# Sketched attention with a phase-mixing MLP on one core: batch 3's queries turned by TensorE, the balance by sums on ScalarE, and a new order of work

## The chip, the core and the metric

The kernel runs on one core of one Trainium2 chip. The metric is the device time of one execution in microseconds (us). A core has five engines that each run their own instructions in order: TensorE (PE; its weight loads are listed apart as PEld), VectorE (DVE), ScalarE (ACT), GpSimd (POOL) and SyncE (SP, whose queue starts most of the transfers). An engine waits where an instruction needs something that another engine or a transfer has not finished; everything behind it on the same engine waits too.

## The reference

For each of 4 batches with 4 heads, 1088 tokens and 32 values per head:

```
phi(x)  = outer(S1 x, S2 x)              8 x 8 values per token
kv, z   = sum over tokens of phi(k) v^T, of phi(k)
x       = (phi(q) kv) / (phi(q) z + 1e-6)       heads side by side: 1088 x 128
theta   = x @ w_theta
y       = w_tok_r @ (x cos theta) + w_tok_i @ (x sin theta)    w_tok: 1088 x 1088
u       = x + y
out     = u + relu(u @ w_ch)
```

q, k, v are float32. The four w matrices come in float64, and the kernel reads their bits.

## The kernel before

**Stages.** k is rounded into two parts and summed into kv and z (batches 0, 1, then 2 and 3 together). q is loaded, scaled by a power of two, turned so that tokens lie along the free axis, rounded into f16 and a rest, and multiplied with the sketches (`levels`). VectorE builds denominators and outer products, TensorE makes the numerators, and ScalarE copies them from the accumulators into x, turned (`xT`). Then come theta, cosine and sine (ScalarE with its table), the products zr and zi (VectorE), the mixing with the 17 rows of w_tok (8 real, 8 imaginary, and a tail of both), and the last product with w_ch. Batches 0 and 1 are mixed row by row (`mix_row`, L1193); batches 2 and 3 go through seven products of half size (`winograd`, L1291) with sums and differences made by VectorE.

**Weights.** A row of w_tok is 1088 KB. It is loaded into a buffer of class "zs" (`weight`, L575). ScalarE makes two parts of it (L576 and L578), VectorE shifts one (L316) and adds them with a custom operation (L312). There are only 5 "zs" buffers, which the tiles of x also use.

**Queries.** `load` (L588 to L605) issues one transfer of 576 KB for batches 0 to 2. For batch 3, which stands in `QTURN`, it issues 16 transfers of 36 KB that put blocks of 32 tokens by 32 values in place, so that VectorE's transpose of 32x32 blocks (L944) turns the whole; ScalarE then scales it (L945). For the other batches `query_slices` turns three groups of three 128x128 blocks on TensorE (L951) and ScalarE scales each group out of the accumulator (L954).

**Turning x.** For batches 1 to 3, VectorE transposes xT in 32x32 blocks (L1097), one transfer writes it to memory (`far`, L1098) and four fetch it back (L1102).

**Balance.** Batches 2 and 3 are combined in one scheme, so batch 3 is scaled to batch 2's size by a power of two. `balance` (L1166) finds the largest magnitude in each of the two on VectorE (L1169), `ratio` makes the two powers from them with small VectorE operations, ScalarE scales batch 3 (L1092), and `add` (L1351) takes the scale back.

**Output.** `finish` (L1219) multiplies by w_ch, adds on VectorE, transposes there (L1240) and stores from several queues (L1236). The last part of batch 3's first half goes through `finish_turned` (L1266), which transposes on TensorE (L1274) and stores whole rows (L1286).

**The order.** No scheduler runs when the kernel is built. `ORDER` (L34) lists the numbers of all operations in the order in which they are issued, `GAPS` (L79) says ahead of which of them filler matmuls are put on TensorE (L361, results unused), and `SLOTS` (L80) gives each buffer its place in its class. Within an engine the instructions stand in this order; between engines only the operands decide. Helpers record nearly all matmuls at L332, VectorE's operations at L312, L316 and L319, so a line alone does not name an operation; the tiles do.

Of the kernel before, what the change touches and what calls it, by code (L numbers as in the profile page):

```python
# [18 lines left out]
ALU = mybir.AluOpType  # L19
# [12 lines left out]
RPS = 4  # L32
EARLY = (2, 60.0, 4.0)
ORDER = (  # L34
# [43 lines left out]
)  # L78
GAPS = {11: 3, 57: 3, 79: 3, 110: 1, 203: 8, 153: 1, 77: 5, 86: 2, 163: 1}  # L79
SLOTS = (  # L80
# [11 lines left out]
)  # L92
WARM = 0
LOAD_LEAD = 60.0
RAW_LEAD = 30.0
CHAINS = ((0,), (1,), (2, 3))
QPOOL = (False,) * 4
KEEP = (2, 3)
KEEP_CLS = "big"
PAIR = (2, 3)  # L100
QUADS = (2, 3)
QTURN = (3,)
XTURN = (1, 2, 3)
PARTS = ((0, 384), (384, 544))
APOOL = ()
# [140 lines left out]
def kernel(  # L246
# [81 lines left out]
    def vop(n, fn, w, r, due=None, two=False, lk=0):  # L328
        op("V", dve2(n) if two else dve(n), fn, w, r, due, lk=1 if two else lk)
# [836 lines left out]
    def balance():  # L1166
        at("even")
        for j, b in enumerate(PAIR):
            vop(NC * P, lambda j=j, b=b: V.tensor_reduce(out=even()[:, j:j + 1], in_=xT[b](), axis=AX.X, op=ALU.max,  # L1169
                                                         apply_absolute_value=True), [(even, j)], [xT[b]])  # L1170

        def ratio():
            e = even()
# [309 lines left out]
```

## Time and profile before

| what | value |
|---|---|
| median of 3 runs | 217.91 us (217.88 to 218.24) |
| the profiled execution | 217.77 us |
| its span in the profile | 216.0 us |
| mean granted clock of TensorE | 0.997 |
| read from memory, written | 29.84 MB, 4.00 MB |
| mean transfer rate over the span | 172 GB/s |

The profile shows one execution. Its span runs from the first to the last instruction that it records, and the execution's own time is 1.77 us longer. "Busy" counts the time in which at least one instruction of an engine runs, so overlapping matmuls count once: a group's busy time over its count is less than the mean duration of one. In rows of groups the columns are line, engine, operation, result and operands with their shapes, count, busy time, mean duration in ns, and the idle time just before with what ended it. In rows of the timeline they are start, length, engine, line, operation and count. A digit in the 40 slices is the busy share of a fortieth of the span in tenths.

### The profile page before, as it was taken

How to read it: one execution, taken by the hardware profiler on the slowest of the kernel's cores; microseconds unless marked ns; L12 is line 12 of the kernel's file. 1: busy time of each engine (PE TensorE's matmuls, PEld its weight loads, DVE VectorE, ACT ScalarE, POOL GpSimd, SP SyncE). 2: the span in 40 equal slices, each digit the busy share in tenths (PEclk: the TensorE clock that was granted, in tenths of full speed). 3: DMA queues.
4: the chain of work that ended last, by engine and by line, in shares of the span. 5: the costliest groups of instructions: out<-in, count | busy, mean ns of one | idle time of the engine just before them, and what ended most of it. 6: DMA issues, size and time to landing. Idle time of an engine off the chain costs nothing.

```text
span 216.0 us, 5299 instructions
## 1 busy us (share of the span) xinstructions
PE 207.4 (96%) x2140; PEld 150.2 (70%) x2140; DVE 180.7 (84%) x359; ACT 113.5 (53%) x240; POOL 38.5 (18%) x89
## 2 busy tenths in 40 slices
PE   7999999999999999999999999999999999999990
PEld 7777798968767666775656676576766776677660
DVE  1799999999999998998999999979497799955151
ACT  4899999999999896796711423159500000000000
POOL 1182640307300000930003010000220020020013
PEclk9999999999999999999999999999999999999998
DMA  6999999996996994192002244022660012110433
GB/s 226 395 417 418 380 362 420 429 324 143 347 244 230 421 429 177 56 323 49 0 0 36 40 141 113 0 39 108 137 109 0 0 39 50 17 36 4 76 62 67
DMA packets 28044, 37.06 MB, mean 172 GB/s; under 512 B 20564, under 2 KB 23044, under 8 KB 25844
## 3 DMA queue, kind: packets, MB, share of 16 engines
q1 hardware_dynamic: 22868, 31.86, 42.2%
q0 software_dynamic: 1552, 3.25, 7.1%
q10 hardware_dynamic: 3600, 1.62, 2.8%
q8 instruction: 17, 0.28, 0.5%
q14 instruction: 7, 0.06, 0.1%
HBM read 29.84 MB, written 4.00 MB: 157 GB/s over the span
## 4 chain that ended last, share of the span: by engine, by line
PE 58%; DMA 17%; DVE 10%; ACT 9%; issue 3%; SPq 1%; POOL 0%; POOLq 0%; DVEq 0%; ACTq 0%
PE ps L332 54%; DMA zs<-w_tok 11%; DMA zs<-far 2%; DMA st<-s 2%; DVE big L312 2%; ACT big L578 2%; PE ps L951 2%; ACT big L626 2%; DMA far<-zs 1%; DVE g L312 1%; PE ps L1053 1%; DVE big L316 1%; ACT g L726 1%; ACT big L576 1%; PE ps L361 1%
## 5 line engine op out<-in xcount | busy, mean ns | idle before, releaser
L332 PE MATMUL ps<-big,zs 128*128 128x384 f32 (+2 forms) x380 | 108.8, 435 | 0.0
L332 PEld LDWEIGHTS ps<-big,zs 128*128 128x128 f32 x380 | 67.1, 191 | 34.2 <-issue 0.9
L1281 ACT COPY g<-ps 80x256 f32<-80x256 f32 x1 | 0.4, 367 | 54.1 <-PE ps L1274 54.1
L332 PE MATMUL ps<-big,big 128*32 128x32 f32 (+2 forms) x352 | 21.8, 235 | 0.0
L312 DVE CUSTOM_DVE_ANT_0 big<-big,big 128x2176 uint16<-128x2176 uint16 x17 | 21.6, 1281 | 0.1
L578 ACT ACTIVATE big<-zs 128x1088 int32<-128x1088 uint32 (+1 forms) x18 | 21.3, 1190 | 0.7 <-DMA zs<-w_tok 0.7
L576 ACT ACTIVATE big<-zs 128x1088 f32<-128x1088 f32 x17 | 20.9, 1229 | 0.7 <-DMA zs<-w_tok 0.7
L332 PEld LDWEIGHTS ps<-big,big 128*32 128x32 f32 (+1 forms) x352 | 14.9, 125 | 5.6 <-issue 1.0
L312 DVE TENSOR_TENSOR big<-big,big 128x544 f32<-128x544 f32 x24 | 16.7, 713 | 0.1
L326 POOL DMA_DIRECT2D g<-big x6 | 5.3, 1070 | 56.0 <-ACT g L1213 56.0
L1236 POOL DMA_DIRECT2D out<-g x8 | 5.0, 631 | 50.3 <-DVE g L1240 36.0
L312 DVE TENSOR_TENSOR zs<-zs,g 128x384 f32<-128x384 f32 (+2 forms) x24 | 9.9, 449 | 4.0 <-DMA zs<-far 4.0
L316 DVE TENSOR_SCALAR big<-big 128x1088 int32<-128x1088 int32 x17 | 12.3, 721 | 0.0
L361 PE MATMUL ps<-idle 128*128 128x112 bf16 (+1 forms) x67 | 10.0, 312 | 1.3 <-POOL idle L363 1.3
L312 DVE TENSOR_TENSOR g<-lv 128x768 f32<-128x768 f32 x12 | 11.1, 950 | 0.1
L312 DVE TENSOR_TENSOR big<-big,hf 128x1152 f32<-128x1152 f32 x8 | 10.7, 1351 | 0.0
L332 PE MATMUL ps<-mf,big 128*128 128x96 f32 (+1 forms) x72 | 10.0, 278 | 0.4 <-DVE big L312 0.4
L332 PE MATMUL ps<-sbk,g 128*128 128x64 f32 x72 | 10.1, 276 | 0.3 <-ACT g L726 0.3
L332 PE MATMUL ps<-w,big 128*128 128x128 f32 (+1 forms) x76 | 10.2, 278 | 0.0
L332 PEld LDWEIGHTS ps<-w,big 128*128 128x128 f32 (+1 forms) x76 | 9.4, 190 | 0.5
L1139 ACT ACTIVATE g<-g 128x384 f32<-128x384 f32 x12 | 6.3, 532 | 6.7 <-DVE g L319 6.7
L332 PEld LDWEIGHTS ps<-sbk,g 128*128 128x128 f32 x72 | 9.0, 191 | 0.8 <-ACT g L726 0.6
(198 smaller groups left out, 353.0 us busy)
## 6 DMA issues: line engine op xcount, KB each, us to landing
zs<-w_tok SPq DMA_DIRECT2D x17, 1088.0 KB, 10.6
big<-k_l SPq DMA_DIRECT2D x5, 576.0 KB, 12.6
big<-v_l SPq DMA_DIRECT2D x4, 576.0 KB, 15.4
big<-q_l SPq DMA_DIRECT2D x3, 576.0 KB, 10.4
big<-hf POOLq DMA_DIRECT2D x3, 576.0 KB, 9.7
far<-zs SPq DMA_DIRECT2D x3, 576.0 KB, 3.8
zs<-far SPq DMA_DIRECT2D x12, 144.0 KB, 4.1
big<-k_l ACTq DMA_DIRECT2D x2, 576.0 KB, 4.2
```

Of the source, the lines that this page charges most:

```text
L312: eng.tensor_tensor(out=o, in0=a, in1=b, op=f)
L316: (eng or V).tensor_scalar(out=o, in0=a, scalar1=s1, scalar2=s2, op0=op0, **kw)
L326: op("G", 0.9, lambda: G.dma_start(dst(), src(), accum_op=ALU.add), w, r, fly=fly)
L332: T.matmul(o, lhs, rhs, start=start, stop=stop, skip_group_check=True)
L361: T.matmul(nowhere()[:, :n], idle()[:, 0:P], idle()[:, :n], start=True, stop=True, skip_group_check=True)
L576: op("A", 0.22 + n * 0.0009, lambda: A.activation(dfn(), words_of(raw(), n)[1].bitcast(F32), AF.Prelu, scale=2.0**-112, alpha=-(2.0**32)), ...
L578: op("A", 0.22 + n * 0.0009, lambda: A.activation(stp(), words_of(raw(), n)[0].bitcast(U32), AF.Copy, scale=2.0**-29), [stp], [raw])
L626: op("A", act(n) + 0.1, lambda: A.activation(flat(r()), kc(), AF.Square, accum_out=km()[:, 1:2]), [r, (km, 1)], [kx])
L726: op("A", act(GW), lambda kT=kT, tr=tr: A.copy(kT().rearrange("p c n -> p (c n)"), tr()), [kT], [tr])
L951: T.transpose(tr()[:, i * P:(i + 1) * P], x()[:, g * GC + i].rearrange("p h d -> p (h d)"), ident())
L1139: op("A", act(GW), lambda cs=cs: A.activation(cs()[:, 0], cs()[:, 1], AF.Abs), [(cs, 0)], [(cs, 1)])
L1236: E.dma_start(out[b, s0:s0 + n, f * SQ:(f + 1) * SQ].rearrange("(c j) i -> j c i", j=SQ), ot()[f * SQ:(f + 1) * SQ, :n].rearrange("j (c i) ...
```

## The change

Three things are changed, and one follows from them.

- `QTURN` is empty: batch 3's queries are loaded in one transfer of 576 KB and turned like those of the other batches, in three groups of three transposes on TensorE with a scaled copy by ScalarE behind each.
- `balance` takes the sum of magnitudes in place of the largest: ScalarE runs Abs over xT with an accumulator, and writes the magnitudes themselves, in bf16, into a buffer of class "hf" that nothing reads.
- `ORDER` and `SLOTS` are new. Operations are numbered anew, as batch 3's load is 1 operation in place of 4 and its turning 6 in place of 2. On every engine the instructions up to about 36 us of the trace stand as before. Behind that, all of the work of batches 0 and 1 up to theta is put ahead of the first mixing product (TensorE's 57.13 us in the trace of before), batch 1's turn of x comes earlier among VectorE's operations, and another part of the output comes last. `GAPS` names the same operations by their new numbers.

The lists cut to their first and last lines, and the rest whole:

```diff
 ORDER = (
-    0, 1, 29, 32, 4, 2, 5, 3, 34, 30, 356, 50, 33, 102, 44, 96, 6, 108, 103, 36, 7, 51, 366, 54, 144, 8, 97, 10, 9,
...
-    964, 988, 995, 921, 905, 996, 922, 997, 994, 1000, 916, 923, 998, 917, 924, 999, 918,
+    0, 1, 29, 32, 4, 2, 5, 3, 34, 30, 357, 47, 33, 99, 41, 93, 6, 105, 100, 36, 7, 48, 367, 51, 141, 8, 94, 10, 9, 11,
...
+    914, 965, 915, 916, 993, 996, 997, 994, 998, 1001, 920, 921, 922, 923, 999, 1000, 924, 925,
 )
-GAPS = {11: 3, 57: 3, 79: 3, 110: 1, 203: 8, 153: 1, 77: 5, 86: 2, 163: 1}
+GAPS = {11: 3, 54: 3, 76: 3, 107: 1, 200: 8, 150: 1, 74: 5, 83: 2, 160: 1}
...
-QTURN = (3,)
+QTURN = ()
...
     def balance():
         at("even")
         for j, b in enumerate(PAIR):
-            vop(NC * P, lambda j=j, b=b: V.tensor_reduce(out=even()[:, j:j + 1], in_=xT[b](), axis=AX.X, op=ALU.max,
-                                                         apply_absolute_value=True), [(even, j)], [xT[b]])
+            dump = buf("hf", (NC * P,), BF16, "dump")
+            op("A", act(NC * P) + 0.1, lambda j=j, b=b, dump=dump: A.activation(
+                dump(), xT[b](), AF.Abs, accum_out=even()[:, j:j + 1]), [dump, (even, j)], [xT[b]])
```

104 rows, old and new, of tables (ORDER, SLOTS) are left out of this document.

## The prediction

> **What bounds the kernel now.** I read the page first: its busy shares, its slices, and the engines of the chain that ended last.
>
> ```profile
> PE 207.4 (96%) x2140; PEld 150.2 (70%) x2140; DVE 180.7 (84%) x359; ACT 113.5 (53%) x240; POOL 38.5 (18%) x89
> PE   7999999999999999999999999999999999999990
> PEclk9999999999999999999999999999999999999998
> PE 58%; DMA 17%; DVE 10%; ACT 9%; issue 3%; SPq 1%; POOL 0%; POOLq 0%; DVEq 0%; ACTq 0%
> ```
>
> TensorE is busy for 207.4 of 216.0 us, in every slice but the first and the last, at the full clock throughout. So the bound is TensorE's own work, and time can be won in three places only: less of that work, the few waits inside it, and what lies behind its last matmul. The waits of TensorE from 18 us on, and then the chain in order of time, say how much there is of each.
>
> ```profile
> PE ps L332 <- DVE big L312: 0.4, 1, 0.4
> PE ps L332 <- ACT sm L783: 0.4, 1, 0.4
> PE ps L332 <- ACT g L726: 0.3, 1, 0.3
> ...
> 88.94 1.30 DVE zs L1097
> 90.25 3.05 DMA far<-zs
> ...
> 94.65 5.14 DMA zs<-far
> ...
> 117.78 90.94 PE ps L332 x515
> 208.94 0.72 PE ps L332 x6
> 210.44 0.52 DVE big L319
> 210.97 0.59 DVE g L1240
> 211.85 0.64 POOL out L1236
> 212.49 0.60 POOLq L1479
> ```
>
> Three idle spells of 0.3 to 0.4 us are all that the waits show, and from 117.78 us the chain is one piece of 515 matmuls. VectorE is nearly as full up to 120 us; the table by stage shows it, with ScalarE in the column behind.
>
> ```profile
> 36.00:57.00 21.00, 21.00 (x498) 17.32 (x488) 20.55 (x45) 20.18 (x49) 7.88 (x17) 1.00 0.92 321
> 57.00:70.00 13.00, 13.00 (x174) 8.58 (x163) 13.00 (x19) 12.34 (x21) 0.00 (x0) 1.00 0.86 247
> 100.00:120.00 20.00, 19.54 (x98) 12.72 (x97) 19.64 (x33) 7.96 (x12) 1.82 (x2) 1.00 0.12 20
> ```
>
> The columns are stretch and length, then PE, PEld, DVE, ACT and POOL busy. From 36 to 70 us VectorE is idle for 0.45 us and ScalarE for 1.5. TensorE is full, VectorE has no room, and whatever order is chosen has to keep both fed from each other.
>
> **The change, part by part.** The rows of the removed work and of its nearest relatives, grouped by form:
>
> ```profile
> L951 PE MATMUL ps<-ident,big 128*128 128x128 f32 x27 | 4.5, 283 | 0.0
> L954 ACT ACTIVATE big<-ps,qs 128x384 f32<-128x384 f32 x9 | 5.0, 602 | 0.0
> L944 DVE STREAM_TRANSPOSE big<-big 128x1152 f32<-128x1152 f32 x1 | 1.4, 1372 | 0.0
> L945 ACT ACTIVATE big<-big,qs 128x1152 f32<-128x1152 f32 x1 | 1.2, 1239 | 0.0
> L1169 DVE TENSOR_REDUCE even<-big 128x1 f32<-128x1152 f32 x2 | 2.7, 1330 | 0.8 <-ACT big L1081 0.8
> L924 ACT ACTIVATE big<-big 128x1152 f32<-128x1152 f32 x4 | 4.7, 1175 | 0.1
> L924 ACT ACTIVATION_READ_ACCUMULATOR big<-big 128x1 f32 x4 | 0.8, 201 | 0.0
> 20.64 0.48 PE ps L951 x3
> ```
>
> *Queries of batch 3 on TensorE.* VectorE loses one transpose, 1.37 us; ScalarE exchanges one copy of 1.24 us for three of 0.60, so +0.56. TensorE gains nine transposes. Their 27 relatives take 4.5 us of busy time, 167 ns each, so 1.5 us; three that stand alone on the chain take 0.48, so 1.44 for nine; between other matmuls the neighbours overlap them, and I know no bound below 1.0. TensorE is the bound and nothing hides them: I take **+1.3 us** (1.0 to 1.5). With no overlap at all it would be nine times the mean of 283 ns, 2.5 us; that stands as a rival below.
>
> [...]
>
> *The load.* Batch 3's queries came in 16 issues of 36 KB, and stand in SP's queue as follows.
>
> ```profile
> 36.75 14.23 SPq L596 DMA_DIRECT2D big<-q_l  x8
> 52.62 12.86 SPq L596 DMA_DIRECT2D big<-q_l  x8
> big<-q_l SPq DMA_DIRECT2D x3, 576.0 KB, 10.4
> big<-q_l SPq DMA_DIRECT2D x16, 36.0 KB, 10.6
> ```
>
> SP spends 27 us of its queue on them, with weight rows behind. One issue of 576 KB replaces them; its like land in 10.4 us. It now waits until TensorE has freed its buffer at about 37 us, and only two weight loads and later ones stand behind it; the data is used on TensorE from about 50 us, so I cost it at nothing. If it landed after 50 us, TensorE would wait from there.
>
> *Balance on ScalarE.* VectorE loses two reductions, 2.66 us; ScalarE gains two passes like L924's, 2 x (1.18 + 0.20) = 2.75 us. They stand behind the copies of the numerators of batches 2 and 3, where ScalarE has 12 us free in 20 (100 to 120 us). VectorE's total falls by 4.0 us and ScalarE's rises by 3.3. As VectorE is not the bound, this is worth what it removes of TensorE's waits, at most.
>
> *The order.* The instruction lists of the two programs agree up to TensorE's instructions at about 36 us, filler matmuls included. From there I added up each engine's list, each instruction at the spacing its form has in the trace of before, and compared when an operand is ready with when it is wanted. These are sums of rows followed by hand. One check is a row of before:
>
> ```profile
> 57.13 3.06 PE L332 MATMUL ps<-big,zs 128*128 128x384 f32 x9
> 78.70 0.25 PE L332 MATMUL ps<-sq,sm 32*32 32x16 f32 x8 [0.37 <-ACT sm L783]
> 117.78 1.33 PE L332 MATMUL ps<-mf,big 128*128 128x96 f32 x10 [0.42 <-DVE big L312]
> 209.49 0.86 PE L332 MATMUL ps<-big,w 128*128 128x384 f32 x2
> ```
>
> The sum puts before's first mixing product at 57.05 us, the row has 57.13. Over the whole list TensorE's sum ends at 207.2 us and the last row at 210.35: 3.2 us more, of which I put 1.4 to long matmuls that drift and 1.8 to waits, the two shown above (0.37, 0.42) and shorter ones whose idle time the profile fills with pipelined ends. Both parts of this split are estimates (waits 0.8 to 3.2).
>
> In the changed kernel all work of batches 0 and 1 up to the phase angles comes ahead of the first mixing product, which the sum puts at 68.7 us without waits, 70.5 with them. No mixing product fills gaps between 36 and 70 us, so TensorE waits where chains pass through VectorE or ScalarE: for the row scale behind the first denominators (wanted at 40.7, ready at 41.6), for the first outer products (0.2), and for batch 1's last numerators (0.2): **+1.35 us** of new waits (0.5 to 3). Behind that every operand is ready by the sums 1 to 2 us before it is wanted, the weight rows and batch 1's x too, so before's **1.8 us** of waits go. What is late next is VectorE, with those 1 to 2 us of slack.
>
> *The end.* Before, the last product is 384 wide, and a VectorE pass, a transpose and two stores issued by POOL one after the other follow it: from 210.35 to the span's end, 5.65 us. In the changed kernel a half of 160 columns comes last, finished by two short transposes, products of 80x256 and one VectorE pass of 0.42 us, with one store on each queue; by the landing of such a store I put this tail at 4.15 us, **-1.5 us** (-2.0 to 0).
>
> **The sum.** Profiled run 217.77 us (216.0 of span, 1.77 around it, which I leave as it is; 0.14 under the median of 217.91): +1.3 transposes +1.35 new waits -1.8 old waits -1.5 tail = -0.65, **217.1 us**. The likeliest case's own range, by the ends of the small terms, is 216.5 to 217.4. A measurement of this kernel can tell about 0.2%, 0.44 us, from no change.
>
> **The rivals.**
> - *The fill runs dry (slower).* Place: TensorE from 41 to 70 us, where seven hand-overs come from VectorE or ScalarE within 1 us of being wanted. If each costs what the longest wait of before cost, 0.42 us, or VectorE lags by its own waits, it is 3 to 4 us instead of 1.35, and 218.8 to 219.8. It decides if the first mixing product starts after 71.5 us. For it: VectorE's 0.45 idle us in this stretch, so no slack to catch up. Against it: VectorE has 1.4 us less to do there.
> - *Batch 1's x comes late (slower).* Its transpose moves from 88.94 to about 69.3 us. From there to use took 11.1 us before (1.3, then 3.05 and 5.14 of transfers with issues between), so 80.4, and 1.0 of VectorE behind it; TensorE wants it at 84.6. It decides if the transpose begins after 72.5 us; each us more is one on TensorE, with all of TensorE's queue behind it. 5 us of lag give 219.
> - *No change.* The tail gives nothing, or the transposes cost 2.5 us: 217.1 + 1.2 to 1.5 = 218.3 to 218.6; halfway, 217.8.
> - *More is won.* VectorE's 4.0 us less lets no wait arise at all: 1.35 less, 215.8; with half of it 216.4.
> - *The scale's change matters.* Sums give another power of two than maxima; the number of instructions behind it stays the same, so it moves no time.
>
> **How the numbers follow.** Forecast 0.36; more won 0.09; so faster 0.45. No change 0.15 (half tail, or dear transposes in part). Slower 0.40: the fill 0.26, batch 1's x or another operand of VectorE with 1 us of slack 0.10, transposes at full price 0.04. The range leaves out the best ends of "more is won" and the worst of both slower cases: 216.2 to 220.0.
>
> **What would show it.** L951 with 36 rows and about 6 us busy; no L944, L945 nor L1169 on VectorE or ScalarE; two Abs passes of about 1.2 us. First mixing product at 70 to 71 us. TensorE's waits naming VectorE or ScalarE between 41 and 70 us, and none beyond 84. The transpose L1097 of batch 1 near 69 us. TensorE's last matmul at 211.0 to 211.3 and 4.2 us behind it. The forecast is wrong if TensorE's busy time rises by over 2 us, if its waits add up to over 3 us, or if the end behind the last matmul stays above 5 us.

## The result, and the profile after

The changed kernel takes 221.62 us (median of 4 runs, 221.22 to 221.85) against 217.92 before: the ratio is 1.0151, with a 95% interval of 1.0124 to 1.0178. The forecast was 217.1 us with a range that ended at 220.0; the sign and the range were both missed. The profiled run took 221.85 us with a span of 220.0, so 4.0 us of span are to be explained.

From the page of the changed kernel, the busy shares, two rows of slices and the engines of the chain:

```profile
PE 211.8 (96%) x2149; PEld 152.2 (69%) x2149; DVE 178.0 (81%) x356; ACT 116.4 (53%) x246; POOL 39.2 (18%) x89
...
DVE  1799999995958999999999798596869987862453
...
PEclk9999999999999999999999999999999999999999
...
PE 89%; issue 4%; DMA 2%; DVE 2%; POOL 1%; ACT 1%; POOLq 0%; SPq 0%; ACTq 0%
```

TensorE is still the bound, at the full clock (a granted 1.00 in the profiled run). VectorE has dips in the 10th and the 12th slice (49.5 to 55 and 60.5 to 66 us), where it was full before. The table by stage, with the same columns as in the prediction, says the same of all engines:

```profile
36.00:57.00 21.00, 18.83 (x459) 15.10 (x457) 17.81 (x42) 17.87 (x48) 8.19 (x13) 1.00 0.79 289
57.00:70.00 13.00, 12.72 (x287) 9.27 (x285) 10.54 (x24) 11.47 (x29) 0.66 (x2) 1.00 0.51 174
```

From 36 to 70 us VectorE is now idle for 5.65 us and ScalarE for 4.66, where it was 0.45 and 1.48; TensorE, which had no idle time there, shows 2.45. TensorE's timeline has the idle spells, the first mixing product and the last matmul:

```profile
39.30 0.24 PE L332 MATMUL ps<-sf,sm 32*32 32x8 f32 x8 [0.65 <-ACT sm L783]
...
47.56 0.33 PE L1053 MATMUL ps<-ident,g 128*128 128x128 f32 x1
49.28 0.44 PE L1053 MATMUL ps<-ident,g 128*128 128x128 f32 x2 [1.39 <-issue]
...
65.34 0.22 PE L332 MATMUL ps<-sq,sm 32*32 32x16 f32 x5 [0.28 <-issue]
...
74.67 1.13 PE L332 MATMUL ps<-big,zs 128*128 128x384 f32 x3
...
216.10 0.60 PE L332 MATMUL ps<-w,big 128*80 128x128 f32 x4
```

The first mixing product starts at 74.67 us; the prediction's sum had 68.7 without waits and 70.5 with them. TensorE ends at 216.70, and 3.34 us follow, where 5.64 followed before. The largest idle spell stands between the first and the second of three transposes, and is put down to "issue": TensorE waited for nothing that the profile shows.

The 4.0 us, sorted by the terms of the prediction's sum (the sums are those of the prediction):

| stretch | before | changed | difference |
|---|---|---|---|
| matmuls in the list, by the sums | 171.05 | 171.96 | +0.9 |
| first mixing product, over its sum | 0.1 | 6.0 | +5.9 |
| from there to TensorE's end, over its sum | 3.1 | 2.6 | -0.5 |
| from TensorE's end to the span's end | 5.64 | 3.34 | -2.3 |

By this sorting the loss lies ahead of the first mixing product. The two lists part earlier than the description of the change and the prediction have it: at 34.0 us on TensorE, 34.7 on VectorE and 33.2 on ScalarE (trace of before), not at 36. TensorE is 0.15 us behind there, and 6.0 over its sum at the first mixing product.

### The profile page after: what moved, and what is told of

The parts are those of the page before. It is cut to its first block, busy times and chain, and to the rows that moved or that the text cites. A ratio compares the mean times of both kernels' runs of the same rounds, so it can differ in the third digit from the quotient of the medians.

```text
span 220.0 us, 5292 instructions
## 1 busy us (share of the span) xinstructions
PE 211.8 (96%) x2149; PEld 152.2 (69%) x2149; DVE 178.0 (81%) x356; ACT 116.4 (53%) x246; POOL 39.2 (18%) x89
## 4 chain that ended last, share of the span: by engine, by line
PE 89%; issue 4%; DMA 2%; DVE 2%; POOL 1%; ACT 1%; POOLq 0%; SPq 0%; ACTq 0%
PE ps L332 80%; PE ps L1053 2%; DMA st<-s 2%; PE ps L951 2%; PE ps L361 2%; PE ps L723 2%; POOL out L1237 1%; DVE big L319 0%; PE ps L1126 0%; DVE hf L316 0%; ACT big L576 0%; POOLq L1480 0%; DVE g L1241 0%; PE ps L896 0%; PE ps L906 0%
## 5 line engine op out<-in xcount | busy, mean ns | idle before, releaser
L1214 ACT COPY g<-ps 128x384 f32<-128x384 f32 (+1 forms) x6 | 2.5, 461 | 20.1 <-PE ps L332 20.1
L319 DVE SCALAR_TENSOR_TENSOR big<-ps,even,big 128x384 f32<-128x384 f32 (+1 forms) x10 | 4.8, 493 | 7.1 <-PE ps L332 7.1
L332 PEld LDWEIGHTS <-hf 128*32 128x32 bf16 (+1 forms) x252 | 7.5, 96 | 3.5 <-issue 1.6
```

What stands on the lines that cost most here:

```text
L319: (eng or V).scalar_tensor_tensor(out=o, in0=a, scalar=s, in1=b, op0=op0, op1=op1)
L332: T.matmul(o, lhs, rhs, start=start, stop=stop, skip_group_check=True)
```

## The experiments

Theory: the new order of the stretch up to the first mixing product costs the time, not the change of the code. Rivals: batch 3's queries cost it; the new order's second half costs it. Then the question is what in that stretch costs the time: TensorE's instruction stream, ScalarE's queue, or the chain's own length. Each ratio below is against executions of the kernel before that were taken beside the run; their medians lie between 218.0 and 218.4 us, so ratios are compared rather than times.

**The old code in the new order.** `QTURN` and `balance` as before, the new `ORDER` and `SLOTS`; the 16 loads stand where the one load stood.

```diff
-QTURN = ()
+QTURN = (3,)
-            op("A", ..., lambda ...: A.activation(dump(), xT[b](), AF.Abs, accum_out=even()[:, j:j + 1]), ...)
+            vop(NC * P, lambda ...: V.tensor_reduce(out=even()[:, j:j + 1], in_=xT[b](), ...), ...)
```

> The new order and slots carried by the old code: batch 3's queries in 16 blocks turned by VectorE, balance by maxima on VectorE, each put where the new order has its counterpart. Theory, the order costs it: TensorE loses about 5 us between 36 us and the first mixing product and gains 2 behind its last matmul, as in the changed kernel, and only the nine transposes (1.1 to 1.3 us) go: 220.0 to 220.6 us. Rival, the queries cost it (nine transposes and their copies in the crowded stretch, the load in one piece): 217 to 218.5 us, first mixing product before 71 us.

Measured: 232.43 us, ratio 1.0644 (1.0600 to 1.0688), first mixing product at 79.78. Neither theory foresaw it. SP's queue and TensorE's two longest waits:

```profile
37.70 15.91 SPq L596 DMA_DIRECT2D big<-q_l  x16
53.71 9.77 SPq L575 DMA_DIRECT2D zs<-w_tok  x3
```

```profile
PE ps L332 <- ACT lv L991: 3.9, 1, 3.9
PE ps L332 <- DVE zs L1043: 2.5, 1, 2.5
```

The 16 issues hold SP's queue for 15.9 us. ScalarE waits 7.3 us, until 55.37, for the last of them to land, because its first pass over these queries (L924) stands ahead of the copy of L991 in its queue; TensorE's 3.9 us are the wait for that copy. The granted clock was lower too, 0.61 between 57 and 70 us of this trace and 0.96 to 0.98 over each of the six runs (0.99 to 1.00 in those of the kernel before beside them), so not all of the loss is waiting. In this place the new order can't be had with the 16 loads; so this run doesn't part the order from the code, and the next one has to.

**The new code in the old order.** One load at the place of the first block load, the six operations of the turning at the place of VectorE's transpose, the balance at its old place; all other operations and buffers as in `ORDER` and `SLOTS` of before.

```diff
-QTURN = (3,)
+QTURN = ()
-            vop(NC * P, lambda ...: V.tensor_reduce(...
+            op("A", ..., lambda ...: A.activation(dump(), xT[b](), AF.Abs, ...
```

> The old order and slots carried by the new code: one load of 576 KB, nine transposes on TensorE where VectorE's transpose stood, balance by sums on ScalarE. Theory, the order costs it: 217.9 plus the transposes, 218.5 to 219.2 us. Rival, the queries cost it: 220.5 us or more. Third, VectorE's 4.0 us less is worth as much as the transposes cost: 217.6 to 218.0 us.

Measured: 217.57 us, ratio 0.9989 (0.9969 to 1.0008). The third expectation holds: the code costs nothing that these runs can tell. TensorE's waits from 18 us on are down to one row:

```profile
PE ps L332 <- ACT g L726: 0.3, 1, 0.3
```

Nine transposes more are in it, and TensorE still ends at 210.19 us, 0.16 earlier than before. Matmul by matmul, TensorE falls 1.0 us behind before at the nine transposes (96.51 to 97.66 us) and has made up 0.9 of it by 117.78 us, where before waited for VectorE's sum. Another 0.4 is made up at 78.70 us; two kernels below that run the old code up to there (the balance alone, and the first with a new end) make up 0.3 and 0.2 of it too, so part of that isn't the change's.

**The balance alone, in the old order.** Only the second pair of lines above.

> The old order and the old way with the queries, only the balance by sums on ScalarE: VectorE loses 2.7 us near 138 to 143 us, TensorE gains nothing. Theory, the new code in the old order came out even because VectorE's relief pays for the transposes, and this is the part of the relief that costs TensorE nothing: 217.2 to 217.7 us. Rival, VectorE's relief at 140 us is off the path and the pay comes from the queries' transpose at 104 us: 217.8 to 218.1 us.

Measured: 218.60 us beside 218.42 of the kernel before, ratio 0.9996 (0.9965 to 1.0026), no difference that these runs can tell, as the rival has it. The wait for VectorE's sum that the prediction quoted (0.42 us) is still there:

```profile
PE ps L332 <- DVE big L312: 0.4, 1, 0.4
```

With the queries changed as well it is gone. What pays for the transposes is thus the change of the queries, and not the 2.7 us of reductions near 140 us. VectorE's transpose of the queries stands at 97.71 us in before, shortly ahead of that wait; as the load and ScalarE's copy changed with it, that it was the transpose alone is not shown.

**Old head, new rest; new head, old rest.** The new code in two mixed orders, buffers given places anew where the two lists collide.

```diff
+ORDER = OLD[:750] + [i for i in NEW if i not in OLD[:750]]
```

```diff
+ORDER = NEW[:748] + [i for i in OLD if i not in NEW[:748]]
```

> The new code; the first 750 of 1002 operations in the old order (up to about the first products of the scheme for batches 2 and 3), the rest in the new one. Theory, all of the loss lies ahead of the changed kernel's first mixing product and its end is truly shorter: first mixing product at 57.2 us, 3.3 to 4.2 us behind TensorE's last matmul, 215.3 to 216.6 us, faster than both kernels. Rival, the new order's second half costs as much as its end gains: 217.3 to 218.0 us.

> The counterpart: the new code, the first 748 operations in the new order and the rest in the old one. Theory: the loss of 5 us ahead of 74.7 us stays and the shorter end goes, 222.5 to 224.0 us, first mixing product at 74 to 75 us. Rival, the loss arises in the second half: 217.5 to 219 us.

Measured: 216.46 us, ratio 0.9903 (0.9874 to 0.9932), for the old head; 223.47 us, ratio 1.0233 (1.0202 to 1.0263), for the new one. Both theories' numbers. The old head's first mixing product and last matmul, then the new head's first mixing product:

```profile
57.24 3.06 PE L332 MATMUL ps<-big,zs 128*128 128x384 f32 x9
...
211.36 0.60 PE L332 MATMUL ps<-w,big 128*80 128x128 f32 x4
```

```profile
74.93 1.46 PE L332 MATMUL ps<-big,zs 128*128 128x384 f32 x4
```

The old head ends 3.34 us behind its last matmul (211.96 to 215.30), as the changed kernel does; the new head with the old end has 5.6 there. (The old head reaches to 96 us of its trace.) So the loss sits in the new order's head, the new end is a gain of its own, and the old head with the new rest beats both kernels. The pages of the new code in the old order, and then of the new head with the old rest, say more. The two have the same code and the same end:

```profile
PE 207.4 (96%) x2149; PEld 150.6 (70%) x2149; DVE 176.7 (82%) x356; ACT 115.9 (54%) x246; POOL 38.5 (18%) x89
```

```profile
PE 211.2 (95%) x2149; PEld 151.8 (68%) x2149; DVE 177.9 (80%) x356; ACT 116.3 (52%) x246; POOL 40.1 (18%) x89
```

The span grows by 6.4 us (215.8 to 222.2). 3.8 of them are busy time of TensorE, with the same 2149 matmuls and granted clocks of 0.995 and 0.994; only the other 2.6 are idle time.

**Is it the instruction stream?** The trace also records transfers of instructions: 17 of 16 KB over the span on one queue (`q8 instruction: 17, 0.28, 0.5%` on the page), taken here for TensorE's. A record is a weight load, a matmul or an instruction of the sequencer; the changed kernel has 4348 of them on TensorE. There the stop at 47.56 us lies at record 1729, and 1729 + 63 is 7 x 256; the spell at 65 us lies at record 2497, and 2497 + 63 is 10 x 256. The two lie 768 records apart, and three of the 16 KB transfers stand between the one that ends at the first stop and the second stop (from 51.93, 55.58 and 63.07 us). So 16 KB seem to be 256 instructions, which is worked out from these two stops. Two runs on that. First, 20 more of the filler matmuls that run while TensorE has no data yet:

```diff
-    op("P", 3.2, lambda: [spin(112) for _ in range(39)], ...
+    op("P", 3.2, lambda: [spin(112) for _ in range(59)], ...
```

> The changed kernel with 20 more of the filler matmuls that stand ahead of the first data, where TensorE is idle from 5.2 to 7.8 us: 40 instruction records more ahead of everything, nothing else. Theory, the stop at 47.6 us is the end of a chunk of 256 instructions (it stands at record 1729, and 1729 + 63 is 7 x 256): it moves to an instruction that stands 40 records earlier in the program, among the small products of batch 2's sums at 46.5 us, still at record 1729, and the three transposes at 47.6 run without a stop. Rival, the stop belongs to those transposes: it stays at them, at record 1769.

```profile
49.21 0.88 PE L1053 MATMUL ps<-ident,g 128*128 128x128 f32 x6
50.02 0.21 PE L332 MATMUL ps<-hf 128*32 128x32 bf16 x5
52.28 0.27 PE L332 MATMUL ps<-hf 128*32 128x32 bf16 x15 [2.05 <-issue]
52.48 0.87 PE L332 MATMUL ps<-g,sm 128*64 128x384 f32 x4
53.28 0.55 PE L1053 MATMUL ps<-ident,g 128*128 128x128 f32 x3
```

The three transposes (the last row) run through, and the stop has moved to the small products, 40 records earlier in the program and again at record 1729. One run, 225.59 us: the shift also put a chunk's end among the fillers at 13 us, where TensorE then stood for 1.6 us, and the granted clock was 0.50 from 24 to 27 us, so its time tells nothing more. The stop is the end of a chunk.

Second, what delays the transfer. Moving one load was the first try (397 is the load of row 9, 382 that of row 6):

```diff
+ORDER.remove(397); ORDER.insert(ORDER.index(382) + 1, 397)
```

> The changed kernel with one thing moved: the load of weight row 9 (1088 KB), issued at 38.3 us and first read at about 80, now stands behind the load of row 6 in SP's queue. The trace of the changed kernel shows TensorE's instruction stream standing still for 1.7 us at 47.6 us in the middle of three transposes that wait for no semaphore, with a 16 KB instruction transfer ending at 47.8. Theory, that transfer queues behind the loads: the stop falls under 0.7 us, time 220.2 to 220.9 us. Rival, the stop has to do with TensorE's own pace through small matmuls: it stays at 1.4 to 1.8 us, time 221.3 to 221.8 us.

Measured: 221.26 us, ratio 1.0150 (1.0120 to 1.0180); the stop was 1.47 us, the rival's number. It was no test of the loads: those ahead of the moved one keep the transfers full until 46 us anyway (share 1.04 from 44 to 46 us). So three loads were cut; this kernel leaves out most of three weight rows, so only its time is of use:

```diff
+        m = 64 if L.stage in ("row5", "row7", "row9") else n
-        op("S", n * 1024 / 380e3, lambda: SY.dma_start(raw(), src), ...
+        op("S", n * 1024 / 380e3, lambda: SY.dma_start(raw()[:, :m], src[:, :m]), ...
```

> The changed kernel with the loads of weight rows 5, 7 and 9 (issued at 23 to 38 us, 1088 KB each) cut to their first 64 columns, which ScalarE then reads 17 times in place of 1088 columns: 3.1 MB of transfers and most of three weight rows are left out, every instruction of the engines stays. Moving row 9 alone had left the transfers full until 46 us. Theory, TensorE's instruction transfers are slowed by the loads: they start under 2 us after TensorE enters the chunk of 256 instructions ahead (3.3 to 3.7 in the changed kernel), the stops at 47.6 and 65 us vanish, first mixing product 1.5 to 2 us earlier, time 219.5 to 220.2 us. Rival, TensorE's own pace: the stop at 47.6 us stays above 1.2 us and the time is 221.2 to 221.8.

Measured: 220.84 us, ratio 1.0094 (1.0066 to 1.0122), the profiled run 220.17 against 221.85; first mixing product at 73.04. The timeline there:

```profile
47.41 0.33 PE L1056 MATMUL ps<-ident,g 128*128 128x128 f32 x1
47.99 0.44 PE L1056 MATMUL ps<-ident,g 128*128 128x128 f32 x2 [0.25 <-issue]
```

The stop between the two starts fell from 1.72 to 0.58 us, and the first mixing product came 1.63 earlier. That is 1.14 at this stop, 0.35 at the stop at 65 us, which is gone, and 0.15 by which TensorE was ahead before either. From 42 to 49 us the DMA share was 0.55 in place of 1.04, and the transfer began 2.7 us behind the entry of the chunk ahead in place of 3.7. So the loads do delay the instructions. The theory was right in kind and too strong: the transfer still starts 2.7 us after the chunk ahead is entered, not under 2, the stop shrinks by two thirds and doesn't vanish, and the median lies above its range. From the traces' records of these transfers (us; "stop" from the start of the last record of one chunk to the first of the next):

```
kernel               TensorE enters   next chunk's         enters the    stop
                     a chunk          transfer             next chunk
before               41.77            45.70 to 46.67       50.27         none
changed              43.11            46.83 to 47.76       49.28         1.72
row 9 moved          43.03            46.56 to 47.51       48.95         1.47
three loads cut      42.96            45.70 to 46.66       47.99         0.58
20 more fillers      44.41            49.84 to 50.89       52.28         2.23
```

Each time the transfer starts 2.7 to 5.4 us after TensorE has entered the chunk ahead of it and takes about 1 us; where TensorE stops, it goes on 1.3 to 1.5 us behind the transfer's end. Before, it needed 8.5 us for these 256 instructions and came to the next chunk 3.6 us behind that end; the changed order brings as many in 4.5 us, and has to wait.

**Is it ScalarE's queue?** Three conversions of weight rows (353, 394, 388) put behind copies that the chains need (331, 339, 189):

```diff
+for a, b in ((353, 331), (394, 339), (388, 189)):
+    ORDER.remove(a); ORDER.insert(ORDER.index(b) + 1, a)
```

> The changed kernel with three conversions of weight rows on ScalarE (1.2 us each, issued at 36 to 48 us) moved behind the small copies that batch 0's and batch 1's chains need, nothing else. Theory, the chain's hand-overs wait in ScalarE's queue behind conversions that nobody needs before 50 us: TensorE's wait for the small copy at 39.3 us (0.65) goes, the first mixing product comes 0.7 to 1.2 us earlier, time 220.3 to 221.0 us. Rival, VectorE's part of the chain is as long, so the wait only changes its name: 221.3 to 221.8 us.

Measured: 221.51 us, ratio 1.0131 (1.0091 to 1.0171): the rival's time. The first mixing product came at 75.39, later than in the changed kernel. The wait at 39.3 us shrank to 0.2, and the profile shows two others:

```profile
PE ps L332 <- ACT g L1057: 1.5, 2, 1.1
PE ps L1053 <- issue: 1.2, 1, 1.2
```

The row of `issue` is the chunk's end, here at 49.16 us. The longest wait put down to L1057, 1.1 us up to 66.05 us, is most likely a chunk's end too: it stands at record 2497, where the changed kernel stops as well, and TensorE goes on 1.45 us behind the end of a 16 KB transfer (63.38 to 64.60). With 20 more fillers, where that record is another instruction, these products show no wait. So the moved conversions gained 0.4 us of waiting at 39.3 us, and lost 0.3 at a hand-over at 46.8 us and 0.8 at a longer stop at the chunk's end; the rival's reason, VectorE's part of the chain, is not shown by this run.

In the changed kernel VectorE and ScalarE do wait from 36 to 75 us, for each other and for TensorE. VectorE's two longest waits, then ScalarE's longest:

```profile
DVE big L316 <- ACT lv L991: 2.3, 1, 2.3
DVE sm L312 <- PE ps L332: 1.9, 2, 1.5
```

```profile
ACT lv L991 <- PE ps L332: 1.5, 1, 1.5
```

These read as one chain through three engines: TensorE's sketch products of batch 1, ScalarE's copy, VectorE's denominators. That it sets the time is not shown: TensorE itself is idle for 2.5 us only. Its starts, taken one by one from the traces, say more. Of the 6.0 us over the sum, 3.1 are four idle spells, counted over the usual spacing: 1.6 and 0.4 at the two ends of chunks, 0.8 at 39.3 us behind ScalarE's small copy, and 0.3 at 42.3 us ahead of the products of the row scale. Everywhere else TensorE is idle for less than 0.1 us at a time, and nearly all starts lie as far apart as like ones in before. But where a matmul of one form is followed by one of another form, the next start comes later than the first form's usual spacing: 0.20 us from a transpose (`128*128 128x128` in the rows) to a product in a tile of `128*32`, 0.13 from a product of `128*32 128x32` back to a tile of `128*128`, 0.42 behind the last of four products of `128*64 128x384`. The changed order has 45 such pairs that before doesn't have. Sums over the list from before's mean spacings put the first mixing product at 67.8 us if these 45 are counted at the first form's mean, near the prediction's 68.7, and at 70.8 if they are counted at what a like change costs in before. Both are estimates from the two traces. So about 2 us more are work that the prediction's sum most likely had too short, and 0.8 stay without a place.

**The end, in the old order.** Two kernels with the 160 wide half of batch 3 last, as in the changed kernel, and then a third with the 384 wide part finished ten products earlier. Where the operations of the last output stand (product 3 and its 384 and 160 wide parts p0, p1; product 4 likewise):

```diff
-old:    ... 4p1  3p1 sum  out p1 (transposes, products)  3p0 sum  out p0 (product, turn, stores)
+first:  ... 3p0 sum  4p1  out p0  last of 3p1  sum  out p1
+second: ... 3p0 sum  4p1  out p0  last three of 3p1  sum  out p1
+third:  ... 3p0 sum  out p0  ten products of 4  last three of 3p1  sum  out p1
```

> The kernel before with only the order of its last 35 operations changed: the 384 wide part of batch 3's first half is finished ahead, and the 160 wide part through the transposes on TensorE comes last, as in the changed kernel. Theory, the new end is worth 2.35 us whatever stands ahead of it (5.65 us from TensorE's last matmul to the end of the span before, 3.3 after): 215.4 to 216.2 us. Rival, the end is bound by the stores' own queue and what is gained behind the last matmul is lost as waits ahead of it: 217.3 to 217.9 us.

> The new code in the old order, with the end in a new order: the 160 wide half of batch 3 comes last through the transposes on TensorE, and three of its products are kept back as filler for the two hand-overs that cost 0.9 and 0.5 us in the end that was tried first. Theory, an end without new waits is worth the shorter tail: TensorE's last matmul at 210.4 to 210.8 us, 3.5 to 4.5 us behind it, 215.7 to 216.7 us. Rival, the waits come back elsewhere: 217.3 to 217.7 us.

> The new code in the old order, with batch 3's 384 wide part finished some ten products ahead of the end, so that its stores and those of the other half leave SP's and POOL's queues before the last ones come. In the end tried before it TensorE was done at 210.6 us, but four stores stood in a row in SP's queue, 0.5 us each, the last issued at 212.7. Theory, the stores' queues set the end: last store issued at most 1.2 us behind the last matmul, 215.5 to 216.4 us. Rival, the end's length is the landing of a store whatever is queued: 217.2 to 217.7 us.

Measured: 217.85 us, ratio 0.9996 (0.9971 to 1.0021) with the old code; 217.67 us, 0.9976 (0.9949 to 1.0003) with the new code and fillers kept back; 217.35 us, 0.9950 (0.9926 to 0.9974) spread. All three times lie in the rivals' ranges; only the third kernel is faster than before by more than its interval. In the second TensorE is done at 210.58 us, but the stores are not; SP's queue there, and then that of the old head with the new rest, whose last matmul ends at 211.96:

```profile
210.18 2.45 SPq L1237 DMA_DIRECT2D out<-g  x5
...
212.73 0.39 SPq L1287 DMA_DIRECT2D out<-g  x1
```

```profile
210.33 2.16 SPq L1237 DMA_DIRECT2D out<-g  x3
...
212.58 0.38 SPq L1287 DMA_DIRECT2D out<-g  x1
```

The last store is issued 2.15 us behind the last matmul in the one and 0.62 in the other. The third try still had it 2.4 behind, five stores in a row. In these traces an end is short where the last matmul comes early and the stores' queues are empty by then. The new order has spread its stores over the last 12 us, and none of my three has so few left at the end; that the spreading is what counts was not tested further.

## Why the prediction was wrong

- *Transposes, +1.3 us.* Right in the main. The group has 36 rows and 6.0 us busy, 1.5 more than before; the sums of the lists rose by 0.9.

```profile
L951 PE MATMUL ps<-ident,big 128*128 128x128 f32 x36 | 6.0, 284 | 0.0
L1170 ACT ACTIVATE hf<-big 128x1152 bf16<-128x1152 f32 x2 | 2.3, 1164 | 0.1
```

  One lasts 284 ns here on the mean, and a further one costs 167 of busy time (36 in 6.0 us), so several in a row cost less than that many times 284 ns.
- *Load and balance at nothing.* Right for the balance (0.9996 alone) and for the load, for which ScalarE waits 0.5 us and TensorE shows no wait. With 16 issues in its place the new order takes 11 us more, at a lower granted clock (0.96 to 0.98).
- *New waits, +1.35 us (0.5 to 3).* This is the step that failed, and with it the sign: TensorE comes to the first mixing product 6.0 us behind the sum's 68.7, 5.9 more than before. (The prediction's own 70.5 for that product leaves 1.8 for waits, where its sum took 1.35.) The place was named in the rival "the fill runs dry", and so was the point from which it decides, a first mixing product after 71.5 us. Its price of 3 to 4 was too low, and its mechanism, TensorE waiting for VectorE or ScalarE, is the smaller part: such hand-overs cost 1.1. That this comes near 1.35 is luck, since 0.8 of it stands at 39.3 us, where the sum had none, and of the three places that it named only the row scale shows a wait, 0.3 in place of 0.9. The ends of instruction chunks cost 2.0, which the sums don't know: they add up how long instructions take and take it for granted that they are there. About 2.1 are, by the estimate above, the sum of 68.7 itself, which comes too early where matmuls of different forms follow one another in an order that before doesn't have; 0.8 stay open. That the chunk ends take part was shown by runs; the rest of the split is read from two traces and was not tested by a run of its own.
- *Old waits, -1.8 us.* Too much in this order: from the first mixing product on the changed kernel is 2.6 us over its sum, against 3.1 before, so 0.5 went, with hardly an idle spell left to show. In the old order the new code is 1.7 over (210.19 - 57.32 against a sum of 151.2, the old one and 1.1 for the transposes), so 1.4 went there; part of that, the wait at 78.70 us, is missing in runs of the old code too.
- *The tail, -1.5 us.* Right in sign and short in size: 2.3. It holds in the old head's kernel too.
- *Rivals.* Batch 1's transpose began at 74.40 us, behind the 72.5 from which the prediction let this rival decide. It cost nothing that the trace shows: what uses x had moved back as well, and TensorE shows no wait for it. "No change" and "more is won" fell with the head.
- *The signs of being wrong.* TensorE's busy time rose by 4.4 us, over the 2 that were named. The waits from 18 us on add up to 2.6 in the profile, under the 3, and none between 41 and 70 us names VectorE or ScalarE: most of the loss is not in what the profile calls waits.

The changed kernel is thus a trade: an end that is 2.3 us shorter, code that costs nothing in the old order, and a head that costs 5.9.

## What to carry to other kernels

An engine that is 96% busy can be slower without waiting: here the same 2149 matmuls took 3.8 us more of TensorE's busy time in another order. When a sum of instructions forecasts a new order, give each change from one form to another its own spacing (0.13 to 0.42 us for the three named above), and not only each form. Where small matmuls run beside full loads, count instructions as well: the stretch that brought 256 records in 4.5 us ran out of them. When the profile puts a wait in the middle of such a stretch down to another engine, look whether the record ends a chunk. Try the halves of a new order apart; here one half was worth keeping.

## What the runs showed of the hardware

In these traces TensorE's instructions came in transfers of 16 KB: 17 of them over the span, for 4348 records in the changed kernel, and by the two stops that lie 768 records and three transfers apart a chunk of 256 records each. With the transfers full, up to 47 us in the traces of before and of the changed kernel (DMA share 1.02 to 1.03 from 8 us on in both), the transfer for the next chunk began 2.7 to 4.1 us after TensorE entered the one ahead of it. With few loads in flight it began 1.0 us behind that entry among small matmuls (55.58 and 66.38 us in the changed kernel, share 0.03 from 55 to 57 and 0.04 from 64 to 68), and up to 4.5 us ahead of it among long ones (176.76, share 0.14 from 174 to 182). About 1 us of transfer and, where TensorE stopped, 1.3 to 1.5 us followed. So a chunk that ended in a stop took 6.2 us beside full loads (43.11 to 49.28 us in the changed kernel) and 5.0 with three loads cut (42.96 to 47.99). That is no fixed bound: with 20 more fillers one chunk beside full loads took 4.4 us (39.97 to 44.41), as its successor's transfer began 1.9 us after the entry.

In these two traces the time from one matmul to the next depended on the form of the next: 0.11 us from a transpose to a transpose (the median), 0.20 from a transpose to a product in a tile of `128*32`. The spacings at a change of form were the same in the traces of before and of the changed kernel, within 0.02 us for the three named above (0.20, 0.13 and 0.42), while products in tiles of `128*32` that follow their own kind start 0.01 us apart.
